# Six plain product steps at the start of a fused Fourier-mixing and SiLU kernel

## The chip, the cores and the metric

The kernel runs on one core of a Trainium2 chip. Its time is the device time of one execution in microseconds (us); the medians below are over several executions.

## The reference

The input x has 8 batches of 3008 rows and 256 channels. Each batch is mixed along its rows in the frequency domain, and every row of the result then goes through a two-layer network with SiLU. x, the filters and the result are float32; the two weight matrices come as 64-bit floats.

```python
X = np.fft.rfft(x, axis=1)                       # x: (8, 3008, 256)
Y = X * (filt_r + 1j * filt_i)[None, :, :]       # filters: (1505, 256)
y = np.fft.irfft(Y, n=3008, axis=1)
h = y.reshape(24064, 256) @ w_in                 # w_in: (256, 2048)
g = h * (1.0 / (1.0 + np.exp(-h)))
out = g @ w_out                                  # w_out: (2048, 256)
```

## The kernel before

**The mixing.** The transform of 3008 = 94 x 32 rows is done as products with small tables of cosines and sines, batch by batch. The stages have names that the profile shows as tiles: pa (along the 94), pb (along the 32), the multiplication with the filter, pc (back along the 32), pd (back along the 94), which gives y. Between stages the data is turned by writing it to DRAM and loading it in another order: t (the result of pa) goes out to d1 and comes back as t2, q (the result of pc) goes out to d2 and comes back as t4. Batch 0 is done ahead of everything else, as fast as it goes. The later batches are done in pieces between the products of the network, long before they are needed.

The x of batch 1 is laid out twice: `load_pair` and `stage1_pair` (pa for eight of the 32 columns at a time, four row groups of the array side by side; lines L422 and L432) do parts 0 to 2 ahead of the network, `load_x` and `stage1` (L379, L452) do the last two pieces, u = 6 and 7, in steps 7 and 8. `out_pair` (L445) copies pa out of PSUM, `store_rows` (L465) writes t to d1 with four DMAs of the POOL queue. `store_half` (L720) writes q to d2, `fetch_rows` (L747) loads it for pd, `stage3` (L762, copies L776) is pd of batch 0.

**The network.** The rows are handled in 48 pairs of token blocks; a pair has 8 steps (jp 0 to 7), each for 256 of the 2048 hidden units, so there are 384 steps. A step has the 2 x 2 block form of a matrix product in Winograd's variant of Strassen's scheme: seven products in place of eight at each of the two levels, and sums around them. `hidden(step)` does the first level (products at L1025 into px and pyz): it needs four differences of y, made once for each pair by `tokens` in the tile ty (on VectorE), copies of the running sum px (ScalarE, abc), sums of pyz and abc in g, and Silu (L1029). The last hidden product of a step is followed by a difference of two rows of g, and `finish` adds two more in the next step; all these sums are on VectorE through the helper `combine` (L996). `project(step)` does the second level one step later (L1093, into the accumulators acc 0 to 3, seven products from the rows of g). `drain` adds the accumulators of a pair up in the tile s (copies L1118, then seven sums on POOL), `output` stores them.

A step runs in eight rounds. In a round the generator of `hidden` and the one of `project` each issue up to their next `yield`, then come the pieces that a list has put at this step and round:

```python
for rnd in range(ROUNDS):
    held = work[1:] if rnd in ((3, 6, 7) if keeps else (0, 2) if step in opened else ()) else []
    work = [w for w in work if w in held or next(w, work) is not work]
    until(step + rnd / ROUNDS)
```

The order on each engine is therefore written out by hand. The first 16 steps take two pairs in turn, by `PARTS`: pair 0 with jp 0 and 1 (steps 0 and 1), pair 1 with jp 0 to 3 (steps 2 to 5), pair 0 with jp 2 to 7 (steps 6 to 11), pair 1 with jp 4 to 7 (steps 12 to 15).

**The weights.** They arrive as 16 blocks of 64-bit floats, two blocks for each jp, and are turned into 32-bit floats on the chip while the first steps run: `bits` (two operations of VectorE, L1222 and L1224), `converted` (two of ScalarE, L1231 and L1232), `added`, `signed` and `placed` (one of VectorE each, L1238, L1243, L1250). `combine_weights(jp)` then makes the sums of weight blocks (S1, S2, S3, S4) that the seven products need, in four operations, on VectorE for jp 0 and mostly on POOL for the others. The slot of S3 in `w_t` holds the plain block A21 until then. `weights(j)` issues the load of a block on the SP queue (L1204), into rooms that other tiles leave.

The waits between engines follow from the tiles: whoever takes a buffer over waits for its last reader, and an engine and a DMA queue do their instructions in order.

Of the kernel before, what the change touches and what calls it, by code (L numbers as in the profile page):

```python
# [46 lines left out]
FP32 = mybir.dt.float32  # L47
# [18 lines left out]
LAG = 1  # L66
PARTS = (0, 0, 2), (1, 0, 4), (0, 2, 8), (1, 4, 8)
# [55 lines left out]
def second_pairs(x):  # L123

    rows = np.zeros((96, 32, C), x.dtype)
    rows[0:NR] = x.reshape(NR, 32, C)
    return rows.reshape(3, 32, 4, 4, 2 * C).transpose(2, 3, 1, 0, 4)[0:3].reshape(3, 128, 6 * C)
# [145 lines left out]
def kernel(  # L273
# [96 lines left out]
    def spectral(b):  # L370
# [44 lines left out]
        def load_pair(p):  # L415
# [3 lines left out]
            else:  # L419
                pool, tag = (spool, "s") if p == 1 else (gpool, "g")  # L420
# [4 lines left out]
        def stage1_pair(p):  # L425
# [8 lines left out]
            if p == 2:  # L434
                t = s1pool.tile([128, 2, 2, 2, C], FP32, name=f"t1_{b}_{p}", tag="s1")
                t = [t[:, i] for i in range(2)]
            else:
                pool, tag = (tpool, "t") if p else (typool, "ty")
# [23 lines left out]
        def store_rows(u):  # L462
            t1 = us.pop(("t1", u))
            for k in range(4):
                nc.gpsimd.dma_start(out=d1[k // 2, :, k % 2, 4 * u:4 * u + 4],  # L465
                                    in_=t1[32 * k:32 * k + NS].rearrange("p h n c -> p (h n) c"))

# [364 lines left out]
        return dict(us=us, store_half=store_half, load_pair=load_pair, stage1_pair=stage1_pair, out_pair=out_pair, store_rows=store_rows, evict_y=evict_y, halves=halves, load_first=load_first, stage1_first=stage1_first, load_x=load_x, stage1=stage1, reverse_x=reverse_x,  # L832
# [15 lines left out]
    def plan(b, part):  # L848
# [3 lines left out]
        if b == 1:  # L852
            for u in range(6, 8):
                put(at + u - 47, 3, part["stage1"], u)
        else:
# [203 lines left out]

    def finish():  # L1060
# [9 lines left out]

    def project(step):
# [4 lines left out]
        if new:  # L1076
            acc[pair] = {}
        last = step == n_steps - 1 or steps[step + 1][0] != pair

        order = PROJECT  # L1080
# [4 lines left out]
        elif new:  # L1085
# [3 lines left out]
        for c, k, i, h in order:  # L1089
            if i not in acc[pair]:  # L1090
# [3 lines left out]
                             start=(new and h == 0), stop=last, skip_group_check=True)  # L1094
            if last and pair == len(pairs) - 1:
                drain_last(pair, i, h, n, acc[pair])
            elif last and (h == 1 or i == 3):
                drain(pair, i)
            yield
# [3 lines left out]
    def drain(pair, i):  # L1103
        n = pairs[pair][3]
        more = (pair, i) in parts
        if i == 0 and not more:
# [4 lines left out]
        if i < 3:  # L1111
            dst, src = s[:, 2 * i:2 * i + 2, 0:n], acc[pair][i][:, :, 0:n]
        else:
            dst, src = s[:, 6, 0:n], acc.pop(pair)[3][:, 0, 0:n]
        if more:
# [6 lines left out]
        if i < 3:  # L1122
            return
# [431 lines left out]
```

## Time and profile before

| | |
|---|---|
| median of 3 runs | 2499.14 us (2498.75 to 2501.53) |
| the profiled execution | 2500.93 us |
| its span in the profile | 2499.1 us |
| mean granted clock of TensorE | 0.998 |
| PE products of L1093 and L1025 | 5376 records each |
| HBM read and written | 96.06 MB and 81.26 MB, 71 GB/s over the span |

PE is TensorE, PEld its weight loads, DVE is VectorE, ACT is ScalarE, POOL is GpSimd; SPq, ACTq and POOLq are the queues on which these engines issue DMAs. Times in the profile are counted from the start of the span. A product of two float32 matrices appears as two records of PE. Lines (L1025) are those of the kernel before; in the changed kernel they are some lines further down.

### The profile page before, as it was taken

The page shows a single profiled execution, that of the slowest core. Times are in us where ns is not written, and L with a number is a line of the kernel's source. Part 1 is how long each engine was busy: PE and PEld are TensorE (multiplying, and loading weights), DVE is VectorE, ACT ScalarE, POOL GpSimd, SP SyncE. Part 2 cuts the span into 40 slices and gives each one's busy share as a digit, 9 for nine tenths or more (in the row PEclk, how much of TensorE's full clock was granted, in tenths as well). Part 3 has the DMA queues.
Part 4 walks back from the last instruction along what each step waited for, and adds up shares of the span by engine and source line. Part 5 has one row for each costly group of instructions (what it writes and reads, how often), then busy time and mean ns, then how long its engine had stood idle before and what let it go on. Part 6 is the DMA issues. An engine that isn't in the chain of part 4 may idle for free.

```text
span 2499.1 us, 42322 instructions
## 1 busy us (share of the span) xinstructions
PE 2479.1 (99%) x16234; PEld 2125.2 (85%) x16234; DVE 1761.5 (70%) x3593; ACT 1092.3 (44%) x3001; POOL 458.4 (18%) x708
## 2 busy tenths in 40 slices
PE   9999999999999999999999999999999999999999
PEld 6778888888888888888888888889888888888988
DVE  7876677777777777777777867777677767655544
ACT  3634444444444444444444444444444444444443
POOL 4421112112121122211122112211221111101100
PEclk9999999999999999999999999999999999999999
DMA  8433233213242032420333203321142211200000
GB/s 303 147 88 103 67 72 82 72 37 81 60 96 72 23 93 53 114 63 20 82 75 100 55 26 91 79 68 43 35 107 54 56 43 35 63 21 9 17 9 17
DMA packets 139771, 170.68 MB, mean 68 GB/s; under 512 B 21053, under 2 KB 113565, under 8 KB 139037
## 3 DMA queue, kind: packets, MB, share of 16 engines
q1 hardware_dynamic: 115952, 121.15, 18.4%
q0 software_dynamic: 22656, 45.68, 7.0%
q8 instruction: 127, 2.08, 0.3%
q10 hardware_dynamic: 960, 1.16, 0.1%
q14 instruction: 76, 0.61, 0.1%
HBM read 96.06 MB, written 81.26 MB: 71 GB/s over the span
## 4 chain that ended last, share of the span: by engine, by line
PE 96%; DVE 2%; ACT 0%; issue 0%; POOL 0%; DMA 0%; DVEq 0%; POOLq 0%
PE acc L1093 45%; PE px L1025 25%; PE pyz L1025 19%; PE pd L800 1%; PE pf L522 1%; PE pc L618 1%; PE pb L580 1%; DVE g L996 1%; PE pc L696 0%; PE pa L402 0%; PE pb L562 0%; PE pd L762 0%; PE pa L432 0%; PE idle L1322 0%; DVE w_t L1250 0%
## 5 line engine op out<-in xcount | busy, mean ns | idle before, releaser
L1093 PE MATMUL acc<-g,w_t 128*128 128x256 f32 (+1 forms) x5376 | 1508.6, 376 | 3.2 <-ACT o L813 2.5
L1093 PEld LDWEIGHTS acc<-g,w_t 128*128 128x128 f32 x5376 | 1017.1, 190 | 153.5 <-ACT o L813 15.3
L996 DVE TENSOR_TENSOR g<-pyz,abc 128x256 f32<-128x256 f32 (+1 forms) x1152 | 479.6, 416 | 471.3 <-ACT abc L1046 231.4
L996 DVE TENSOR_TENSOR g<-g 128x256 f32<-128x256 f32 (+3 forms) x1152 | 591.2, 513 | 197.1 <-ACT g L1029 184.0
L1025 PE MATMUL px<-ty,w_t 128*128 128x256 f32 (+1 forms) x2304 | 677.5, 376 | 1.0 <-DVE ty L996 0.5
L1029 ACT ACTIVATE g<-g 128x256 f32<-128x256 f32 (+1 forms) x1152 | 472.8, 411 | 242.5 <-DVE g L996 242.5
L996 POOL TENSOR_TENSOR s<-s 128x256 f32<-128x256 f32 (+1 forms) x329 | 252.3, 784 | 1403.6 <-DVE s L1118 1044.8
L1025 PEld LDWEIGHTS px<-ty,w_t 128*128 128x128 f32 x2304 | 435.5, 190 | 55.9 <-issue 1.8
L1025 PE MATMUL pyz<-y,w_t 128*128 128x256 f32 (+1 forms) x1536 | 453.0, 377 | 6.6 <-DVE g L996 6.4
L1025 PEld LDWEIGHTS pyz<-y,w_t 128*128 128x128 f32 x1536 | 283.0, 190 | 52.9 <-DVE g L996 12.1
L1040 ACT COPY abc<-px 128x256 f32<-128x256 f32 (+1 forms) x384 | 141.3, 368 | 371.2 <-PE px L1025 371.2
L1046 ACT COPY abc<-px 128x256 f32<-128x256 f32 (+1 forms) x384 | 141.4, 368 | 311.6 <-PE px L1025 311.5
L1029 ACT ACTIVATE g<-px 128x256 f32<-128x256 f32 (+1 forms) x384 | 145.7, 380 | 299.3 <-PE px L1025 299.3
L1025 PE MATMUL px<-y,w_t 128*128 128x256 f32 (+1 forms) x768 | 227.8, 378 | 1.2 <-ACT g L1029 1.1
L1025 PE MATMUL pyz<-ty,w_t 128*128 128x256 f32 (+1 forms) x768 | 226.0, 376 | 0.0
L1025 PEld LDWEIGHTS px<-y,w_t 128*128 128x128 f32 x768 | 143.4, 189 | 24.9 <-ACT g L1029 3.9
L1025 PEld LDWEIGHTS pyz<-ty,w_t 128*128 128x128 f32 x768 | 142.5, 190 | 20.8 <-DVE g L996 0.6
L1033 ACT COPY abc<-px 128x256 f32<-128x256 f32 (+1 forms) x384 | 135.1, 352 | 35.2 <-PE px L1025 35.0
L542 POOL DMA_DIRECT2D d<-tf x96 | 48.7, 507 | 212.9 <-DVE tf L472 212.9
L1118 ACT COPY s<-acc 128x512 f32<-128x512 f32 (+1 forms) x94 | 54.2, 577 | 47.3 <-issue 28.5
L639 POOL DMA_DIRECT2D d<-low x36 | 22.1, 614 | 285.8 <-DVE low L635 275.1
L512 DVE TENSOR_TENSOR uf<-x_all 120x512 f32<-120x512 f32 (+1 forms) x72 | 60.2, 864 | 0.3 <-issue 0.3
(133 smaller groups left out, 1364.3 us busy)
## 6 DMA issues: line engine op xcount, KB each, us to landing
t<-d SPq DMA_DIRECT2D x84, 256.0 KB
t<-d SPq DMA_DIRECT2D x224, 96.0 KB
out_dram<-s SPq DMA_DIRECT2D x64, 256.0 KB
d<-q POOLq DMA_DIRECT2D x48, 256.0 KB, 5.2
x_all<-in_x_dram SPq DMA_DIRECT2D x96, 96.0 KB
x_all<-xr SPq DMA_DIRECT2D x96, 96.0 KB
d<-tf POOLq DMA_DIRECT2D x96, 96.0 KB, 2.7
d<-tq POOLq DMA_DIRECT2D x96, 96.0 KB, 2.8
```

The costliest lines, as they stand in the source:

```text
L512: nc.vector.tensor_tensor(out=out, in0=in0, in1=in1, op=op)
L522: nc.tensor.matmul(out=ps[q][32 * k:32 * k + 32], lhsT=wq_t[rows, k], rhs=rhs[k][rows], start=True, stop=True)
L542: nc.gpsimd.dma_start(out=d1[par, :, grp, at:at + 4], in_=part[rows].rearrange("p q n c -> p (q n) c"))
L580: nc.tensor.matmul(out=ps[k, ri][32 * j:32 * j + 32, a, :], lhsT=dn_t[rows, 4 * (g + a) + at, :], rhs=t2s[g + a][rows, at, :], start=True, ...
L996: eng.tensor_tensor(out=out, in0=in0, in1=in1, op=op)
L1025: nc.tensor.matmul(out=out, lhsT=w_t[:, jp, c, 0], rhs=rhs, start=start, stop=True, skip_group_check=True)
L1029: nc.scalar.activation(out=g[:, k, 0:n], in_=g[:, k, 0:n] if src is None else src, func=AFT.Silu)
L1033: nc.scalar.copy(out=sums[:, 0, 0:n], in_=xo)
L1040: nc.scalar.copy(out=sums[:, 1, 0:n], in_=xo)
L1046: nc.scalar.copy(out=sums[:, 2, 0:n], in_=xo)
L1093: nc.tensor.matmul(out=acc[pair][i][:, h, 0:n], lhsT=w_t[:, jp, OUT_PLACE.get(c, c), 1], rhs=g[:, k, 0:n], start=(new and h == 0), stop=la ...
L1118: copy(out=dst, in_=src)
```

## The change

- Steps 0 to 5 use a plain form: `hidden_plain` has eight products a step, two for each of four outputs, and Silu from PSUM; it needs no ty, no abc and no sum on VectorE. Their `project` has eight products in the order of `PROJECT_PLAIN`, from four rows of g. `drain` handles the banks that only one of the two forms fills, and an eighth sum on POOL joins the two forms.
- All of pa of batch 1 is done ahead of the network: `load_pair(3)` and `stage1_pair(3)` take the place of `load_x(6)`, `load_x(7)` and the two `stage1`; the products of part 3 stand between the second and the third group of pd.
- t is stored behind pd: a copy on POOL into `gate` waits for the last eviction of pd, and all stores of t, with those of q, follow it; parts 0 and 3 are stored in four DMAs of twice the size.
- Loads and tiles change place for that: x of part 2 is loaded later, into the room of part 1 before, weight block 3 later, blocks 4 and 5 before pd, block 6 behind it; t of part 3 uses a buffer of g, x of part 3 the other.
- The conversion of weights is spread anew over steps 0 to 8; `combine_weights` is done by VectorE throughout, its order changed so that A21 stays until the plain steps have used it. `tokens(0)` moves from ahead of step 0 to step 4, `tokens(1)` from step 1 to step 11.

```diff
+PLAIN = 6
...
-                pool, tag = (spool, "s") if p == 1 else (gpool, "g")
+                pool, tag = (spool, "s") if p == 2 else (gpool, "g")
...
+        def store_pair(p):
+            t1 = us.pop(("t1", "pair", p))
+            for k in range(4):
+                nc.gpsimd.dma_start(out=d1[k // 2, :, k % 2, 8 * p:8 * p + 8],
+                                    in_=t1[32 * k:32 * k + NS].rearrange("p a h n c -> p (a h n) c"))
...
-        if b == 1:
-            for u in range(6, 8):
-                put(at + u - 47, 3, part["stage1"], u)
-        else:
+        if b > 1:
...
+    def hidden_plain(step):
+        pair, jp = steps[step]
+        n, yt = pairs[pair][3], channels(pair)
+        px = xps.tile([128, 2, 256], FP32, name=f"px_{step}", tag="x")
+        pyz = xps.tile([128, 2, 256], FP32, name=f"pyz_{step}", tag="yz")
+        g = gpool.tile([128, 8, 256], FP32, name=f"g_{step}", tag="g")
+        g_t[step] = g
+        for k, ps, h, left, right, cols in ((0, px, 0, A11, A12, 0), (1, pyz, 0, A11, A12, n),
+                                            (3, px, 1, S3, A22, 0), (2, pyz, 1, S3, A22, n)):
+            for a, c in enumerate((left, right)):
+                nc.tensor.matmul(out=ps[:, h, 0:n], lhsT=w_t[:, jp, c, 0], rhs=yt[:, a, cols:cols + n],
+                                 start=a == 0, stop=a == 1, skip_group_check=True)
+                if a:
+                    nc.scalar.activation(out=g[:, k, 0:n], in_=ps[:, h, 0:n], func=AFT.Silu)
+                if (k, a) != (2, 1):
+                    yield
...
+    PROJECT_PLAIN = [(S3, 0, 3, 0), (S3, 1, 3, 1), (A22, 3, 3, 0), (A22, 2, 3, 1),
+                     (A11, 0, 1, 0), (A12, 3, 1, 0), (A11, 1, 2, 0), (A12, 2, 2, 0)]
...
-        order = PROJECT
+        order = PROJECT_PLAIN if step < PLAIN else PROJECT
...
-        for o, a, b in ((2, 0, 2), (5, 0, 5), (3, 5, 3), (6, 3, 6), (0, 5, 1), (4, 0, 4), (1, 3, 1)):
-            combine(gp, s[:, o, 0:n], s[:, a, 0:n], s[:, b, 0:n], ALU.add)
+        for o, a, b in ((2, 0, 2), (5, 0, 5), (3, 5, 3), (6, 3, 6), (0, 5, 1), (4, 0, 4), (1, 3, 1), (1, 1, 7)):
+            if b < 7 or (pair, 3, 1) in parts:
+                combine(gp, s[:, o, 0:n], s[:, a, 0:n], s[:, b, 0:n], ALU.add)
...
-    second["load_pair"](2)
     tables()
     products(2)
     part["forward"](4)
     inverse(1)
-    weights(3)
+    second["load_pair"](2)
...
     inverse(2)
+    weights(3)
...
-    for u in range(2):
-        second["store_rows"](u)
     second["stage1_pair"](2)
+    second["load_pair"](3)
     added(2)
     signed(0, 1)
     placed(0, 1)
-    combine_weights(0)
...
     added(3)
+    weights(4, 5)
+    idle(4)
+    early[0] += 7
+    part["stage3"](0)
     signed(2, 3)
-    idle(4)
-    part["stage3"](0)
     part["stage3"](1)
-    placed(2)
+    placed(2, 3)
+    second["stage1_pair"](3)
+    out_of(3, 0, 1, copy=act)
+    out_of(3, 2, copy=dve)
     part["stage3"](2)
     part["stage3"](3)
-    placed(3)
-    combine_weights(1, eng=gp)
-    for u in range(4, 6):
+    out_of(3, 3, copy=act)
+    weights(6)
+    gp.tensor_copy(out=gate, in_=y[0, 0][:, 0, 28:29])
+    second["store_pair"](3)
+    for g in (2, 3):
+        for i in range(2):
+            part["store_half"](g, i, 1, gp)
+    second["store_pair"](0)
+    for u in (4, 5, 2, 3):
         second["store_rows"](u)
-    for g in (2, 3, 4, 5, 0, 1):
+    for g in (4, 5, 0, 1):
...
-    weights(4, 5)
-    second["load_x"](6)
-    weights(6)
-    second["load_x"](7)
...
+            (0, 0, (weights, 7, 8)), (0, 1, (bits, 4)), (0, 2, (bits, 5)), (0, 3, (converted, 4), (added, 4)),
+            (0, 4, (added, 5)), (0, 5, (converted, 5)), (0, 6, (signed, 4), (placed, 4)),
+            (1, 0, (signed, 5), (placed, 5), (weights, 9, 10)), (1, 1, (combine_weights, 2, 0)),
+            (1, 2, (bits, 6), (added, 6)), (1, 3, (converted, 6)), (1, 4, (bits, 7), (added, 7)),
+            (1, 6, (signed, 6), (placed, 6), (converted, 7)), (2, 0, (signed, 7), (placed, 7), (weights, 11)),
...
-        step, rnd = combines[pair % per] if pair not in (1, 2) else ((1, 5), (12, 1))[pair - 1]
+        step, rnd = combines[pair % per] if pair > 2 else ((4, 3), (11, 1), (12, 1))[pair]
...
-            work.append(hidden(step))
+            work.append(hidden_plain(step) if step < PLAIN else hidden(step))
```

## The prediction

> **What bounds the kernel now.** I read the busy totals first, then the waits of TensorE, then its instructions in order of time from 40 to 160 us, then the same stretch for the other engines and the queues. Totals (engine, busy us, share, instructions):
>
> ```profile
> span 2499.1 us, 42322 instructions
> PE 2479.1 (99%) x16234; PEld 2125.2 (85%) x16234; DVE 1761.5 (70%) x3593; ACT 1092.3 (44%) x3001; POOL 458.4 (18%) x708
> ```
>
> TensorE (PE) is the bound, so a time comes off only where PE waits, runs slowly, or has less to do. All that the change touches runs before about 160 us. PE in order of time there (start, duration, line, operation; in brackets the idle time before it and its releaser):
>
> ```profile
> 50.31 3.92 PE L762 MATMUL pd<-wi_t,w_t 64*64 64x47 f32 x244
> 55.56 0.44 PE L762 MATMUL pd<-wi_t,w_t 64*64 64x47 f32 x12 [1.33 <-issue]
> ...
> 56.74 0.77 PE L1025 MATMUL px<-y,w_t 128*128 128x256 f32 x2
> 57.30 1.06 PE L1025 MATMUL pyz<-y,w_t 128*128 128x256 f32 x2
> 58.86 1.19 PE L1025 MATMUL px<-ty,w_t 128*128 128x256 f32 x2 [0.50 <-DVE ty L996]
> ...
> 64.20 0.70 PE L1025 MATMUL px<-y,w_t 128*128 128x256 f32 x2
> ...
> 72.44 0.70 PE L1025 MATMUL pyz<-y,w_t 128*128 128x256 f32 x2 [1.07 <-DVE g L996]
> ...
> 108.25 1.88 PE L452 MATMUL pa<-x_all,wx_t 96*128 96x512 f32 x4
> ...
> 130.47 0.70 PE L1025 MATMUL pyz<-y,w_t 128*128 128x256 f32 x2 [1.26 <-DVE g L996]
> ```
>
> One product is two records; from 64.73 us on, products start every 0.4325 us. Step 0 begins at 56.74, step 1 at 64.20: 7.46 us for seven products that need 3.03. The windows of one microsecond say why (busy us of PE, weight loads, DVE, ACT, POOL; then the granted clock, DMA share, GB/s):
>
> ```profile
> 56.00:57.00 1.00, 0.90 (x4) 0.52 (x4) 0.96 (x2) 0.45 (x1) 0.08 (x1) 1.00 0.63 180
> 58.00:59.00 1.00, 0.50 (x2) 0.17 (x2) 0.96 (x2) 0.00 (x0) 0.92 (x2) 0.50 0.97 344
> 63.00:64.00 1.00, 1.00 (x4) 0.67 (x3) 0.58 (x2) 0.24 (x1) 1.00 (x3) 0.50 1.01 303
> 64.00:65.00 1.00, 1.00 (x6) 0.73 (x5) 0.42 (x1) 0.59 (x3) 0.81 (x2) 0.99 1.11 279
> ```
>
> The clock is halved for all of step 0, and step 0 also waits for ty and for the ladder of copies of px. Later the waits are for VectorE (DVE), which does level sums and weight conversion together: it is busy 9.42 of the 10 us from 120 to 130.
>
> **A ledger to one marker.** The marker is the first hidden product of step 12, at 147.29. From 56.74 that is 90.55 us: 163 products (84 hidden, 79 of project) x 0.4325 = 70.5; two pa products of batch 1 at L452, 1.72 each = 3.4; two pd, one pb and their edges, 3.6. The other 13.0 are losses. By starts of steps (64.20, 70.34, 77.73, 84.34, 90.77, 97.36, 104.70, 112.73, 120.81, 128.09, 135.76) they are: step 0 4.4; step 1 0.1; step 2 1.3; steps 3 to 5 1.45; step 6 1.3; steps 7 and 8 0.55; steps 9 and 10 2.8; step 11 1.0.
>
> **Part 1, more products: +5.2.** Steps 0 to 5 get one hidden and one project product each: 12 x 0.4325.
>
> **Part 2, pa: -0.7.** The two pairs at L452 leave (-3.4). One more product of four row groups goes between pd 1 and pd 2. The three at L432 take 41.01 to 49.23, so 2.74 each. It needs its x, whose load (768 KB) now waits until DVE has placed weights 0 and 1, at 47.8. The nearest row is the first four loads of the kernel, of the same size: issued from 1.14, the first product that reads one starts at 6.28, about 5.0 us later. So x lands at about 52.6, pd 1 ends at 52.5, and I put the wait at 0.2 (0 to 1.5). The evictions of pa 2 that it needs end at 50.6 on ACT.
>
> **Part 3, the stall in pd: -1.3.** PE waited twice for nothing that the profile shows: 1.26 before 37.69, and the 1.33 above. Between them lie 381 matmul records and as many weight loads. If that is a block of instructions that came late, it was there at 55.56. In the changed program the same count is reached in the middle of pd 3, at about 56.8 (52.5 + 0.2 + 2.74 + 1.07 for pd 2 + 0.3), so nothing waits. If the block comes later still because the new load and weights 4 and 5 (1.8 MB) run then, up to 1.3 remains. [...]
>
> Step 0 so starts at 56.74 + 2.74 + 0.2 - 1.33 = 58.35.
>
> **Part 4, the losses of steps 0 to 11: 13.0 become 2.3.** A plain step needs nothing from DVE and no ty: each output is two products and a Silu of 0.42.
> - Clock: the fall to 0.50 at 57.4 came 3.2 us after the stall of 54.24. Without the stall PE has one gap of 0.7 ahead of step 0, so I take full clock. [...]
> - Step 0: its eight products take 3.46, but ACT converts weight 4 (two operations, 1.4) between its second and third Silu, and step 1's first product waits for that third one: 0.65.
> - Step 1 and 2: ACT's first Silu of step 1 writes a g buffer that held t of the last pa, so it waits for the store of it. POOL issues that store only after the last eviction of pd (about 58.3), four DMAs at 0.53: 58.8 to 60.9. Landing: 3.0 us is the median of such stores, 6.4 the worst row (issued 61.3, released POOL at 67.70). PE needs this Silu 7.6 us into step 0, at 66: no wait at the median. Behind these stores on POOL come those of q of groups 2 and 3, in whose room weight 7 is loaded: 62.0 + 2.5 landed, +0.5 issue, +4 load: 69. Then DVE's bits, ACT's conversion and the last Silu of step 1 follow; PE needs weight 7 by about 68.9. I put 0.4 (0 to 4).
> - Steps 2 to 5: DVE has for each weight 2 x 0.34 + 3 x 0.60 = 2.5, and 0.35 for each sum of weights, which leaves POOL (24 sums at 0.888 there go). With drains and ty that is 5.5 to 6.6 us of a step's 6.93. ACT has 4 x 0.42 + 2 x 1.4 = 4.5. It fits, with under 1.5 us of slack on the path bits, conversion, Silu: 0.5.
> - Steps 6 to 11: only weights 14 and 15 and two to three sets of sums are left, so DVE has 3.9 to 5.7 us of work in 6.06: 0.2 at the change of form, 0.5 for the rest.
> So 0.65 + 0.4 + 0.5 + 0.7 = 2.25, that is -10.7.
>
> **Part 5, what costs nothing.** The loads of x for pa 2 and of weight 3 go behind q stores on SP: each some 3 to 4 us later, but needed only at 46.5 and 43.0, and weight 3's load, issued at 36.3, should land by 41. Were it late, DVE's evictions of pa would be, 1 us at most. The stores of t leave POOL at 46 to 56 and free the queues for the rows of pd. All 36 POOL issues (19 us) should be done by 85; ty 0 is needed at 96, t2 and t4 at 130. POOL's eighth sum for pairs 0 and 1 (0.82) lies in POOL's idle time. After the marker the drains of pair 0 are shorter on DVE; the wait of 1.10 at 155.23 halves: -0.5.
>
> **Sum:** +5.2 - 0.7 + 0.2 - 1.3 - 10.7 - 0.5 = -7.8. The profiled execution took 2500.93 with a span of 2499.1; the median shown is 2499.14, so it was 1.8 above. Applied to the median: **2491.3 us**; a profile of the same kind would have a span near 2491.3.
>
> **Rivals.** (a) Start as before: the block still comes late, or the stall has another cause; 1.3 stays, the clock halves, and step 0's eight products take 6.9 in place of 3.5: 2491.3 + 1.3 + 3.4 = 2496.0. For it: those 1.8 MB on the queues from 48 to 56. Against: pa 3 gives the fetch 2.74 us. Chance 0.14. (b) The waits come back in the conversion: stores land at 6.4, weight 7 is 4 us late, or DVE and ACT do not keep step (at the 0.75 that the same weight operations took beside POOL, a step's DVE work is 7.5, 0.6 over, five times): 2494.3 to 2494.9 (+3.6, or +3.0). For it: the queues are full from 58 to 68 (shares 0.75 to 1.11). Chance 0.17. (c) Slower: the half clock stays on. It lasted 6.6 us in which PE was 0.5 to 1.0 busy with gaps of 0.5; the plain steps tie every second product to a Silu behind conversions on ACT, and if such gaps recur in steps 0 to 2, their 40 products cost 17.3 more: 2508.6. It decides once PE has a gap of about half a microsecond in each three. Against: the waits I count are 0.65 and 0.4 in 20 us. Chance 0.10. (d) The change does not do what it says, since the conversion and not the levels' sums held PE, and it only moves: DVE full, the losses of steps 1 to 11 stay (8.6, in place of the 1.6 that I leave them): 2491.3 + 7.0 = 2498.3. Against: DVE's five operations on g leave it, some 2.5 us a step. Chance 0.07. My forecast keeps 0.52.
>
> **Numbers.** The forecast's own range, with every unknown at its good or bad end, is 2488.5 to 2494. For eight in ten I add (a) and (b): 2488.5 to 2497.0. A measurement of this kernel can tell 0.2%, 5.0 us. Faster by more (below 2494.1): the forecast and half of (b), which lies on the bound, 0.60. Within: (a), the rest of (b) and (d), 0.30. Slower: (c), 0.10.
>
> **What would show it.** Right: step 0 starts near 58.4, granted clock 1.00 from 56 to 66, no "issue" wait in pd, plain steps 6.9 to 7.1 us apart, the first product of step 12 near 140, waits of PE on DVE below 1 us before it. Wrong: a clock of 0.50 near 60 (a, c), a wait of Silu on DMA d<-t or of DVE on raw (b), DVE over 9 of 10 us with PE waiting for Silu (d).

## The result: slower by 0.3%, and where the time went

The changed kernel takes 2508.79 us in the median of 11 runs (2503.17 to 2512.78), the kernel before 2500.49 beside it (2498.75 to 2502.42): a ratio of 1.0032, 95% interval 1.0023 to 1.0042. The forecast was 2491.3 and faster; its range ended at 2497.0. The profiled execution took 2512.07 us with a span of 2509.9, near the upper end of its runs, so two more were profiled (r1: 2510.03, r2: 2508.54); they show the same two waits.

The totals of the profile after (engine, busy us, share, instructions), with the queue that brings instructions:

```profile
span 2509.9 us, 42292 instructions
PE 2487.4 (99%) x16274; PEld 2129.7 (85%) x16274; DVE 1751.2 (70%) x3582; ACT 1086.4 (43%) x2984; POOL 435.7 (17%) x680
...
q8 instruction: 128, 2.10, 0.3%
```

PE in order of time in the changed kernel (start, duration, line, operation; in brackets the idle time before it and what ended it):

```profile
48.77 3.33 PE L433 MATMUL pa<-x,wx 32*128 32x512 f32 x22 [0.61 <-ACT t L447]
...
59.58 0.67 PE L770 MATMUL pd<-wi_t,w_t 64*64 64x47 f32 x12 [3.87 <-issue]
60.17 5.35 PE L433 MATMUL pa<-x,wx 32*128 32x512 f32 x24
65.45 2.14 PE L770 MATMUL pd<-wi_t,w_t 64*64 64x47 f32 x128
68.38 1.10 PE L1076 MATMUL px<-y,w_t 128*128 128x256 f32 x4 [0.16 <-DVE y L784]
...
77.47 0.70 PE L1076 MATMUL px<-y,w_t 128*128 128x256 f32 x2 [1.30 <-ACT g L1079]
87.68 1.22 PE L1076 MATMUL pyz<-y,w_t 128*128 128x256 f32 x2 [4.76 <-ACT g L1079]
...
119.17 0.70 PE L1030 MATMUL px<-ty,w_t 128*128 128x256 f32 x2 [1.12 <-ACT abc L1038]
```

Two places carry most of the loss. Inside pd, after 116 records, PE stands still for 3.87 us with nothing to wait for that the profile knows ("issue"); before, it was 1.33 us, after 244 records. In step 2, PE waits 4.76 us for a Silu. Behind each wait the granted clock is 0.50: pa 3 takes 5.35 us (the others take 2.86 at full clock, with their overlap), and from 87.68 to 92.76 six rows take 5.08 us that need 2.6. The windows of one microsecond (busy us of PE, weight loads, DVE, ACT, POOL; then the granted clock, the share of the DMA engines' time in use, GB/s) show the first:

```profile
56.00:57.00 1.00, 0.00 (x0) 0.00 (x0) 0.00 (x0) 0.00 (x0) 0.00 (x0) 1.00 0.92 369
58.00:59.00 1.00, 0.00 (x0) 0.00 (x0) 0.00 (x0) 0.00 (x0) 0.00 (x0) 0.71 0.02 8
60.00:61.00 1.00, 1.00 (x12) 0.60 (x10) 0.68 (x2) 0.47 (x1) 0.00 (x0) 0.50 0.07 16
```

From 56 to 59 no engine of the core works: first the DMA engines are full, then they too are idle, and PE still does not go on.

The second place, on the other engines:

```profile
71.19 2.17 POOL L728 DMA_DIRECT2D d<-q  x4
77.62 26.15 SPq L1235 DMA_DIRECT2D raw<-in_moe_w_dram  x9
85.36 0.49 DVE L1253 TENSOR_SCALAR e<-raw 128x512 uint32<-128x512 uint32 x1 [7.37 <-DMA raw<-in_moe_w_dram]
85.88 0.72 ACT L1262 ACTIVATE e<-e,bias_t 128x512 f32<-128x512 uint32 x1 [6.43 <-DVE e L1253]
```

POOL stores q at 71.2, SP may load weight 7 into its room at 77.6, DVE gets it at 85.4, ACT converts it, and behind that conversion on ACT stands the Silu for which PE waits.

**The ledger.** The first hidden product of step 12 comes at 158.64, where the forecast had 139.9. 10.0 of these 18.7 us are there when step 0 begins (68.38, forecast 58.35): the stall 3.9, the half clock in pa 3 2.5, 1.9 more than before between the start of pa and the end of pa 2, 0.9 by which pa of batch 1 began later than before, and 0.4 ahead of pd make 9.6. The other 8.7 lie in steps 0 to 11: 90.26 us where the forecast had 81.55. There the waits 0.38, 1.30, 4.76 and 1.12 and the half clock of 2.5 make 10.1, against 2.25 of losses in the forecast; the last 0.9 is spread over small gaps. Behind the marker 2351.3 us remain (2351.8 before): the half microsecond that was forecast.

### The profile page after: what moved, and what is told of

Same layout as the page of the kernel before. It is cut to its first block, busy times and chain, and to the rows that moved or that the text cites. A ratio compares the mean times of both kernels' runs of the same rounds, so it can differ in the third digit from the quotient of the medians.

```text
span 2509.9 us, 42292 instructions
## 1 busy us (share of the span) xinstructions
PE 2487.4 (99%) x16274; PEld 2129.7 (85%) x16274; DVE 1751.2 (70%) x3582; ACT 1086.4 (43%) x2984; POOL 435.7 (17%) x680
## 4 chain that ended last, share of the span: by engine, by line
PE 96%; DVE 1%; DMA 1%; ACT 1%; issue 0%; POOL 0%; SPq 0%; DVEq 0%
PE acc L1122 45%; PE px L1030 25%; PE pyz L1030 19%; PE pd L808 1%; PE pf L530 1%; PE pc L626 1%; PE pb L588 1%; PE pa L403 1%; DMA d<-q 0%; PE pc L704 0%; PE pb L570 0%; PE pd L770 0%; DMA raw<-in_moe_w_dram 0%; DVE g L1001 0%; PE pc L684 0%
## 5 line engine op out<-in xcount | busy, mean ns | idle before, releaser
L1001 DVE TENSOR_TENSOR g<-pyz,abc 128x256 f32<-128x256 f32 (+1 forms) x1134 | 471.8, 416 | 473.5 <-ACT abc L1051 230.7
L1001 DVE TENSOR_TENSOR g<-g 128x512 f32<-128x512 f32 (+1 forms) x1134 | 581.8, 513 | 193.7 <-ACT g L1034 180.8
L1030 PE MATMUL px<-ty,w_t 128*128 128x256 f32 (+1 forms) x2268 | 664.8, 375 | 1.1 <-ACT abc L1038 1.1
L1034 ACT ACTIVATE g<-g 128x256 f32<-128x256 f32 (+1 forms) x1134 | 465.4, 410 | 232.7 <-DVE g L1001 232.7
L1030 PEld LDWEIGHTS px<-ty,w_t 128*128 128x128 f32 x2268 | 427.5, 190 | 53.8 <-ACT abc L1038 1.5
L1030 PE MATMUL pyz<-y,w_t 128*128 128x256 f32 (+1 forms) x1512 | 443.9, 375 | 1.3 <-DVE g L1001 1.1
L1045 ACT COPY abc<-px 128x256 f32<-128x256 f32 (+1 forms) x378 | 139.2, 368 | 368.0 <-PE px L1030 368.0
L1051 ACT COPY abc<-px 128x256 f32<-128x256 f32 (+1 forms) x378 | 139.2, 368 | 309.3 <-PE px L1030 309.1
L1038 ACT COPY abc<-px 128x256 f32<-128x256 f32 (+1 forms) x378 | 132.9, 352 | 33.7 <-PE px L1030 33.7
L1150 ACT COPY s<-acc 128x512 f32<-128x512 f32 (+2 forms) x96 | 54.5, 568 | 49.3 <-issue 27.8
```

The costliest lines, as they stand in the source:

```text
L1001: eng.tensor_tensor(out=out, in0=in0, in1=in1, op=op)
L1030: nc.tensor.matmul(out=out, lhsT=w_t[:, jp, c, 0], rhs=rhs, start=start, stop=True, skip_group_check=True)
L1034: nc.scalar.activation(out=g[:, k, 0:n], in_=g[:, k, 0:n] if src is None else src, func=AFT.Silu)
L1038: nc.scalar.copy(out=sums[:, 0, 0:n], in_=xo)
L1045: nc.scalar.copy(out=sums[:, 1, 0:n], in_=xo)
L1051: nc.scalar.copy(out=sums[:, 2, 0:n], in_=xo)
```

## The experiments

Three theories and their rivals were tried. A: the stall in pd is a block of PE's instructions that comes late because loads fill the DMA engines; the half clock follows. B, its rival: the stall belongs to the count of instructions, whatever is loaded. C: step 2 waits because weight 7 must wait for the stores of q, which POOL issues too late. E: the moved loads of x of pa 2 and of weight 3 are not free. All edits are against the changed kernel, unless said otherwise; times are medians and ratios are against the kernel before, which had 2500.8 to 2501.3 beside them.

**e1, weights 4 and 5 behind pd.**

```diff
-    weights(4, 5)
     idle(4)
...
     out_of(3, 3, copy=act)
+    weights(4, 5)
     weights(6)
```

> The changed kernel with the loads of weights 4 and 5 (1.0 MB) issued behind pd, where weight 6 is issued, and not ahead of it. Theory A (the stall of 3.87 us inside pd is the block of instructions coming late because the loads ahead of pd fill the DMA engines; the half clock behind it follows from the stall): the stall falls to 1.3 us or less, the products of pa 3 take about 2.8 us and not 5.35, and step 0 starts at 62.5 to 64.5, not 68.4; the whole some 4 to 6 us shorter than the changed kernel's 2508.8, about 2503.5. Rival B (the stall belongs to the count of instructions and not to the loads): a wait of 3 to 4 us stays at the 117th product of pd, half clock behind it, step 0 at about 68.4, time within 1.5 us of 2508.8. Either way the wait of 4.76 us in step 2 should stay.

2511.68 us, ratio 1.0041 (1.0029 to 1.0054); the stall is 3.61 us. That looks like B, but the edit had no effect: SP issued these loads at 55.04, right behind the end of pa 2 (54.98), as in the changed kernel (52.17 behind 52.10), since nothing that SP waits for stands between the two places (weight 4 waits for the room of x of pa 2, in either order). Here the place in the program delayed the loads only by what their queue waits for. e1 says nothing on A.

**e2, stores of q of groups 2 and 3 ahead of the gate.**

```diff
+    for g in (2, 3):
+        for i in range(2):
+            part["store_half"](g, i, 1, gp)
     gp.tensor_copy(out=gate, in_=y[0, 0][:, 0, 28:29])
     second["store_pair"](3)
-    for g in (2, 3):
-        for i in range(2):
-            part["store_half"](g, i, 1, gp)
```

> The changed kernel with the four stores of q of groups 2 and 3 issued on POOL ahead of the gate on y and of the store of the last pair, not behind them. Theory C (the load of weight 7 waits in SP's queue for these stores, its conversion stands ahead of a Silu on ACT, and so step 2 waits 4.76 us and the clock halves again): the load of weight 7 is issued some 7 us earlier, the wait in step 2 falls below 1 us, no half clock from 87 to 92, and the time is about 6 us shorter than 2508.8: 2502 to 2504. Rival D (what makes weight 7 late is the queue of transfers itself, or the store of t that step 1's g waits for): the load moves, but the wait in step 2 stays above 3 us, and the time within 2 us of 2508.8. The stall in pd stays at 3.9 us with its half clock either way.

2505.82 us, 1.0023 (1.0014 to 1.0032). Weight 7 is issued at 65.8 and the wait in step 2 is gone, as C has it. Part of it is back in step 1 (3.12 us, where the changed kernel has 1.30): g has the buffer of the last t there and waits for its store. That weight 7, now loaded beside this store, makes it slow was not shown:

```profile
76.96 1.22 PE L1076 MATMUL px<-y,w_t 128*128 128x256 f32 x2 [3.12 <-ACT g L1079]
```

And against the expectation, this profile has no stall in pd at all, though it has the same instructions on PE and the same loads. Its pa 2 waits 2.42 us instead, and the clock is halved from 49.1 to 59.3; weights 4 and 5, which wait for the end of pa 2, go out only at 55.4.

**e3, both edits.**

> Both edits together: the loads of weights 4 and 5 behind pd, the stores of q of groups 2 and 3 ahead of the gate. By theories A and C the gains add up: 10 to 12 us under the changed kernel, 2497 to 2499, at or a little under the kernel before (2500.5). By B and D nothing changes, about 2508. If the two are one chain (a step 0 that starts earlier finds weight 7 later still), the sum is 3 us or more below the two gains.

2506.95 us, 1.0023 (1.0014 to 1.0032); the profiled run took 2501.97. Again no stall in pd, and 2.85 us of wait in step 1. The gains of 10 to 12 us did not come: e1's half of the edit does nothing, and e2's gives part of its gain back. That two variants had no stall opened a new question: is it there in every execution? The list of the DMA queues by quarters of a microsecond answers what the waits can't: queue 8 brings PE's instructions in packets of 16 KB (2.10 MB in 128 packets for 32548 records of PE and weight loads, so 254 for each), and one sees when each packet ran (times of packets are the starts of these quarters). In the changed kernel the packet in question ran at 57.00, in the kernel before (its 1.33 us) at 53.00, in e2 at 53.75, in e3 at 53.50. The queues of the changed kernel from 51 to 57, then from 57.00 to 57.25 (packets, MB, share; q1 has the loads that SP issues):

```profile
q1 hardware_dynamic: 648, 2.00, 99.6%
q10 hardware_dynamic: 41, 0.03, 2.5%
```

```profile
q1 hardware_dynamic: 16, 0.03, 30.1%
q8 instruction: 1, 0.02, 27.4%
```

For six microseconds the loads have the engines almost to themselves; the packet comes as they end. In e2 it ran ahead of the issue of weights 4 and 5, in e3 0.6 us behind it (52.9).

**e4, the kernel before with weights 4 and 5 ahead of pd.**

```diff
     signed(2, 3)
+    weights(4, 5)
     idle(4)
...
-    weights(4, 5)
     second["load_x"](6)
```

> The kernel before with one edit: the loads of weights 4 and 5 issued ahead of pd. Theory A: its stall in pd (1.33 us, at the 245th product) grows to 2.5 us or more, or another comes at the 117th product, half clock in or behind it for 5 us or more; time 1 to 5 us above 2500.5. Rival B: the stall stays at 1.3 us and at its place; time within 1.5 us of 2500.5.

2504.08 us, 1.0016 (1.0007 to 1.0025). The stall grew from 1.33 to 3.17 us at its old place, with half clock behind it, as before; the packet ran at 57.00 and not at 53.00. Of these 4 us, 2.0 are a later start of this execution (pa of batch 1 begins at 43.03, before at 41.01). So the stall changes with the loads, with the count of instructions as it was: A, and not B, by one profile and a median 3.3 us above the kernel before. In what way is not plain: the data of the loads had nearly ended by 55, and the packet ran beside stores of t (59% of the engines' time in its quarter).

```profile
59.42 0.66 PE L762 MATMUL pd<-wi_t,w_t 64*64 64x47 f32 x12 [3.17 <-issue]
```

**e5, the loads in the old order.**

```diff
     weights(2)
+    second["load_pair"](2)
     tables()
...
     inverse(1)
-    second["load_pair"](2)
+    weights(3)
...
     inverse(2)
-    weights(3)
```

> The changed kernel with the loads of x of pa 2 and of weight 3 back at their earlier places in SP's queue. Theory E (the prediction's 'costs nothing' was wrong: the moved loads delay the stores of q, the fetch that ACT waits for before it copies pa, and so pa 2): the fetch on ACT is issued some 3 us earlier, the wait of pa 2 for the copies of t (0.6 us in the changed kernel, 1.9 to 2.4 in e1 to e3) goes, and pa 2 starts 1 to 2 us earlier; 1 to 2 us off the 2508.8. But by theory A the block inside pd still waits for the end of the traffic, so the stall is as long or longer and step 0 starts no earlier: then the time stays within 1.5 us. Rival: pa 2 is held by something else, and nothing moves.

2507.06 us, 1.0022 (1.0013 to 1.0031). E holds: no wait in pa 2, and from the first pa to the first pd 9.7 us, where the changed kernel had 11.6 (before: 9.3). All eight profiles with the new order of loads show this wait, 0.3 to 2.4 us; none with the old order does. As A had it, the packet still comes after the loads (55.75) and the stall is longer, 4.72; against the expectation, step 0 begins 2.0 us earlier than in the changed kernel (66.40, there 68.38). The medians are 1.7 us apart, and their intervals overlap. The lines of pd:

```profile
51.42 2.07 PE L770 MATMUL pd<-wi_t,w_t 64*64 64x47 f32 x116
58.21 0.66 PE L770 MATMUL pd<-wi_t,w_t 64*64 64x47 f32 x12 [4.72 <-issue]
```

The old order has a price too: a stall of 0.7 to 1.3 us in pc at about 38 us, in all ten of its profiles (that of the kernel before is the first, 1.26), and in none of the new order. There too a packet (36.0 in e5, 35.0 in the changed kernel) ran later beside these loads.

**e8, weights 4, 5 and 6 behind the load of wi,** which truly waits for pd.

```diff
-    weights(4, 5)
     idle(4)
...
-    weights(6)
...
     nc.sync.dma_start(out=wi_t, in_=wi_dram.ap())
+    weights(4, 5)
+    weights(6)
```

> The changed kernel with the loads of weights 4, 5 and 6 issued behind the load of wi, which waits for the last product of pd; in e1 the loads were still issued at 55.0 us, so e1 took nothing away from ahead of pd. Theory A: the packet of 16 KB that brings the next instructions of PE lands by about 54 and not at 57.0; no wait inside pd of over 1.3 us in this profile, full clock in pa 3, step 0 at 61 to 64. What comes back: weight 4 is converted in step 0 and lands 3 to 4 us after step 0 begins, so a Silu of step 0 or 1 waits 2 to 4 us, and the stores of t and q collide with these loads, so the wait for g in step 1 and the one in step 2 grow by 1 to 3 us: 2503 to 2508. Rival B (count alone): the wait of 3.9 us inside pd stays, and the time is 2509 to 2514.

2507.4 us, 1.0022 (1.0013 to 1.0031). No stall, the packet at 52.50, full clock in pa 3, step 0 at 61.77, as A had it. And all of it given back: waits of 3.18 and 0.41 in step 1, since weight 4 is now late, and of 2.66 in step 2.

**e9, the old order of loads, and the stores held only until the first copy of pa 3.**

```diff
-    gp.tensor_copy(out=gate, in_=y[0, 0][:, 0, 28:29])
-    second["store_pair"](3)
+    gp.tensor_copy(out=gate, in_=second["us"]["t1", 6][:, 0, 0, 0:1])
     for g in (2, 3):
         for i in range(2):
             part["store_half"](g, i, 1, gp)
+    second["store_pair"](3)
```

with the edit of e5.

> The changed kernel with the old order of loads (as in e5) and, on POOL, the stores of q of groups 2 and 3 and then of the last pair held back only until the first copy of pa 3 (about 61 us, when the DMA engines were idle), not until pd is done. Theory C: weight 7 loads some 5 us earlier and the stores of t land some 3 us earlier, so the waits of step 1 (1.30, and 3.12 in e2) and step 2 (4.76) are both under 1 us, with no half clock from 87 to 92; step 0 to the first hidden product of step 12 takes 82 to 84 us, not 90.3. The stall inside pd stays (theory A), 2 to 4 us with half clock behind it where it falls so. Time 2500 to 2503. Rival: the waits of steps 1 and 2 belong to the plain form itself (buffers of g) and stay: 2506 to 2509.

2498.96 us, 0.9988 (0.9979 to 0.9997): under the kernel before, and 8.1 us under e5, from which only the stores part it. From step 0 to step 12 it takes 83.3 us (68.70 to 151.97), as C had it: the waits of steps 1 and 2 are 1.44 and none, and the clock is 1.00 from 86 to 94. The profiled execution was its longest (2505.32), with the longest stall of all, 5.22 us.

**e10, e9 and e8 together.**

> e9, and the loads of weights 4, 5 and 6 behind the load of wi as in e8. If A and C both hold and weight 4 is not too late: no stall inside pd, full clock, step 0 at 59 to 61, and 83 to 87 us from there to step 12 (weight 4 and weight 7 now load behind one another, so one Silu wait of 2 to 4 us is expected back): 2494 to 2499, below the kernel before (2500.8). If the weights behind wi cost more than the stall did, it is slower than e9.

2502.74 us, 1.0006 (0.9997 to 1.0015). The stall is down to 1.66, the clock full, step 0 at 61.84; but weight 4 comes late and holds a Silu as in e8, and half clock follows from 69 to 75. The last branch of the expectation: the weights behind wi cost more than the stall.

```profile
55.76 0.44 PE L770 MATMUL pd<-wi_t,w_t 64*64 64x47 f32 x12 [1.66 <-issue]
...
69.15 1.22 PE L1076 MATMUL px<-y,w_t 128*128 128x256 f32 x2 [3.62 <-ACT g L1079]
```

**e12, e9 with weights 4 and 5 issued from ACT in the middle of pd.**

```diff
-    weights(4, 5)
     idle(4)
...
     part["stage3"](1)
+    weights(4, 5, queue=nc.scalar)
```

> e9, with the loads of weights 4 and 5 issued from ACT behind the copies of y of the second quarter of pd (about 56.5 us): behind the packet of instructions that e8 and e10 had at 52.5 and 53.3, and still some 5 us ahead of their conversion in step 0. Theories A and C: the wait inside pd is at most 1.7 us, as in e10, with full clock in pa 3; step 0 at 59 to 62; no wait over 1.5 us in steps 0 to 2; 82 to 84 us from step 0 to the first hidden product of step 12, which then comes at 142 to 145 (147.3 in the kernel before). Time 2494 to 2497, below e9 (2499.0) and the kernel before (2501.3). Rival: the next block of instructions, asked for at about 56, now waits for these loads, and a wait of 2 us or more comes in the second half of pd: 2498 to 2501.

2499.3 us, 0.9986 (0.9978 to 0.9995). No stall at the old place (packet at 51.00). But the rival came too, at half its size: the next packet ran at 58.25, and 1.02 us of stall, where the rival had 2 or more, comes in the second half of pd. The 2494 to 2497 that were expected were missed. In step 1 g waits again for the store of t, which was issued from 62.9 on and released ACT at 72.9:

```profile
60.80 0.80 PE L770 MATMUL pd<-wi_t,w_t 64*64 64x47 f32 x36 [1.02 <-issue]
...
73.38 0.70 PE L1076 MATMUL px<-y,w_t 128*128 128x256 f32 x2 [3.07 <-ACT g L1079]
```

**e14, the stores of e9 alone.**

> The changed kernel with the order of stores of e9 alone: q of groups 2 and 3 and then the last pair, held until the first copy of pa 3; the loads as in the changed kernel. Theory C by itself: the wait of 4.76 us in step 2 and the half clock behind it go, 6 to 8 us off the 2508.8: 2501 to 2503. Rival: the 8 us between e5 and e9 came only together with the order of loads; then 2505 or more.

2503.15 us, 1.0002 (0.9994 to 1.0011), 5.6 under the changed kernel: C by itself, a little less than expected. The wait of 4.76 in step 2 and its half clock are gone; the stall (2.99) and the half clock in pa 3 (5.50) stay.

**e7, the plain form alone:** e12, with pa 6 and 7 of the second batch in the steps again.

```diff
-    second["load_pair"](3)
...
-    early[0] += 7
...
-    second["stage1_pair"](3)
-    out_of(3, 0, 1, copy=act)
-    out_of(3, 2, copy=dve)
...
-    out_of(3, 3, copy=act)
-    weights(6)
-    gp.tensor_copy(out=gate, in_=second["us"]["t1", 6][:, 0, 0, 0:1])
+    gp.tensor_copy(out=gate, in_=y[0, 0][:, 0, 4:5])
...
-    second["store_pair"](3)
...
     nc.sync.dma_start(out=wi_t, in_=wi_dram.ap())
+    second["load_x"](6)
+    weights(6)
+    second["load_x"](7)
...
-        if b > 1:
+        if b == 1:
+            for u in range(6, 8):
+                put(at + u - 47, 3, part["stage1"], u)
+        else:
```

> e12 without the second part of the change: pa 6 and 7 of the second batch are made in the steps, as in the kernel before, and there is no last pair to store. What is left of the change is the plain form of steps 0 to 5. The prediction priced pa in pd at 0.7 us less than in the steps, and charged it a wait of 0.2: then e7 is 0 to 2 us above e12, 2495 to 2499, and the wait for g in step 1 (for the store of t) is gone. Rival: pa 3 inside pd costs more than it brings, since its x is 0.8 MB of the traffic that holds the block of instructions up; then e7 is 1 to 3 us below e12.

2501.36 us, 1.0000 (0.9991 to 1.0008). That is 2.1 above e12, a little over the 0 to 2 expected, so pa 3 in pd seems worth its place. But e7 also loads weight 6 behind wi, and what it shows of the plain form alone is no more than that nothing is left of its gain in this arrangement: its steps wait 0.39, 1.69 and 1.97 us for Silus that stand behind conversions (DVE waits 2.37 and 2.44 for weights that landed late), and pd has two short stalls (0.66 and 1.59). The wait for the store of t is gone, as expected.

**e13, e12 with weights 7 and 8 issued late in step 0.**

```diff
-            (0, 0, (weights, 7, 8)), (0, 1, (bits, 4)), ...
+            (0, 1, (bits, 4)), ...
-            (0, 6, (signed, 4), (placed, 4)),
+            (0, 6, (signed, 4), (placed, 4), (lambda: weights(7, 8, queue=nc.scalar),)),
```

> e12, with the loads of weights 7 and 8 issued from ACT late in step 0 (about 68 us) and not at its start from SP (62.8 in e12). In e12 step 1 waited 3.07 us, since its g has the buffer of the last pair of t, whose store was issued at 62.9 and landed at 72.9 beside these loads. If the store is slow because of them, it lands by 69, the wait in step 1 falls below 1.5 us and the time by 1.5 to 3 us: 2496 to 2498. If the store is slow for another reason (weight 6, its own form), the wait stays near 3 us and the time within 1 us of e12. Should weight 7 land after 81, step 2 gets a wait of its own.

2500.87 us, 0.9998 (0.9989 to 1.0007). The wait in step 1 is cut up (1.50 and 0.71), but the store of t still releases ACT only at 72.27, and the two issues take time on ACT (an issue there took 0.46 and 0.61 us in the changed kernel, at 42.60 and 47.48). This does not clear the loads: with 7 and 8 out of its queue, SP issued weights 9 and 10, which are of the same size, at 62.0 and 62.5 in their place (in e12 at 63.9 and 64.9). What makes this store slow stays open.

**r1 and r2, the changed kernel again; r3 and r4, e9 again.**

> The changed kernel unchanged, a second profiled execution. Its runs lie between 2503.2 and 2512.8 us. If the late block of instructions is what parts them, an execution near 2504 shows no wait inside pd or one under 1.5 us, with full clock in pa 3, and one near 2510 the wait of 3 to 5 us; the wait of 4.8 us in step 2 is in both.

> The changed kernel unchanged, a third profiled execution: as for the second.

> e9 unchanged, a second profiled execution; the first, at 2505.3, was its slowest run, with 5.2 us of wait inside pd. One near 2497 should show that wait 3 us or more shorter, or the half clock behind it gone; the waits of steps 1 and 2 under 1.5 us as before.

> e9 unchanged, a third profiled execution: as for the second.

r1 (2510.03) and r2 (2508.54) have the stall, 3.85 and 3.25 us, with packets at 54.25 and 57.00, and step 2's wait, 5.17 and 4.51. r2 has no half clock in pa 3. No execution near 2504 was among them, so whether the stall parts the runs of the changed kernel was not seen. r3 and r4 (2495.80, 2495.68) have no stall in pd: their packets ran at 48.25 and 48.00, some 0.8 us after x of pa 3 was issued and ahead of weights 4 and 5 (49.1 and 48.9). The longest and the shortest execution of e9, the same program, first the one of 2505.32, then r4:

```profile
60.29 0.67 PE L770 MATMUL pd<-wi_t,w_t 64*64 64x47 f32 x12 [5.22 <-issue]
...
68.70 1.10 PE L1076 MATMUL px<-y,w_t 128*128 128x256 f32 x4 [0.16 <-DVE y L784]
```

```profile
49.95 2.23 PE L770 MATMUL pd<-wi_t,w_t 64*64 64x47 f32 x128
52.98 2.86 PE L433 MATMUL pa<-x,wx 32*128 32x512 f32 x24 [0.80 <-DMA x<-in_x_second_dram]
...
58.70 1.10 PE L1076 MATMUL px<-y,w_t 128*128 128x256 f32 x4 [0.16 <-DVE y L784]
```

Their 9.6 us are all there when step 0 begins, at 68.70 and at 58.70: among them 5.2 of stall, 2.1 of half clock in pa 3, and 2.7 by which pa of batch 1 began later (43.23 and 40.53). The packet of r4, from 48.00 to 48.25, did not need empty queues:

```profile
q10 hardware_dynamic: 39, 0.03, 56.9%
q1 hardware_dynamic: 15, 0.03, 48.7%
q8 instruction: 1, 0.02, 29.0%
```

The packets side by side (us; "end of pa 2" is the end of its last product; the block before begins some 0.6 to 1.0 us ahead of that):

| run | packet | end of pa 2 | PE goes on | stall | step 0 |
|---|---|---|---|---|---|
| changed | 57.00 | 52.10 | 59.58 | 3.87 | 68.38 |
| r1 | 54.25 | 49.62 | 56.90 | 3.85 | 65.97 |
| e5 | 55.75 | 50.28 | 58.21 | 4.72 | 66.40 |
| e9, longest | 57.75 | 51.62 | 60.29 | 5.22 | 68.70 |
| e10 (weights behind wi) | 53.25 | 50.88 | 55.76 | 1.66 | 61.84 |
| e12 (weights held) | 51.00 | 51.15 | | none | 62.37 |
| r4 (e9, shortest) | 48.00 | 48.81 | | none | 58.70 |

From the quarter of the packet to the next product it is 2.5 to 2.7 us in each row with a stall (2.56 for the 1.33 us of the kernel before). Where the packet runs near the end of pa 2, the block is there in time; where it runs 4.5 to 6.1 us later (all profiles), PE stands for about 3 us or more. With weights 4 and 5 loaded ahead in the changed kernel, seven of eleven profiles have the late packet, which ran as the data of these loads ended; in the other four it ran ahead of their issue (e2, r3, r4) or 0.6 us behind it (e3). With these loads held back (e7, e8, e10, e12, e13) no stall is over 1.7 us.

## Why the prediction failed, step by step

**Part 1 (more products)** stands: the plain steps that nothing disturbs are 6.9 us apart, as sixteen products of 0.4325 need.

**Part 2 (pa)** was probably right in its sign: e7 against e12 gives 2.1 us in the medians, where 0.5 was counted, but the two intervals just overlap and e7 differs in more than pa. The wait for x is 0.80 where it can be seen (r4), inside its 0 to 1.5; from issue to product it is 5.7 us there (47.26 to 52.98), where the forecast took 5.0.

**Part 3 (the stall) is the step that failed first.** Its reading of the stall, a block of instructions that came late, fits every run, and so does the count: the stalls of pc and pd lie at only three places in the order of PE's products, 253 and 128 apart, which with as many weight loads is two blocks and one of the 254 records that a packet brings here (some records are missing). The inference was wrong: "in the changed program the same count is reached at about 56.8, so nothing waits" took the time 55.56 of the one block that was late before as if blocks came by the clock. Each block is brought by a packet of its own (127 of them in the profile before, 128 after). In the kernel before, the block ahead of it had come at 49.25, while stores of t and the rows for pd were moving (DMA share 0.92); in the changed one that block, 128 products and their weight loads earlier, had to come while 1.8 MB of x and weights were moving, and it came at 57.0. The sentence after it ("if the block comes later still because the new load and weights 4 and 5 run then, up to 1.3 remains") named the cause and then bounded it by the old stall: the bound should have been the end of that traffic, about 57, plus the 2.5 us that the old stall could have shown (53.00 to 55.56). The term was -1.3; it measured +2.5, and +2.5 of half clock with it. That these loads bring the packet late is shown by e4 (57.00, before 53.00) and by the runs with the loads held back (no stall over 1.7 us); in what way they do is open. Where the block is in time, the step is right: r4 starts step 0 at 58.70, forecast 58.35.

**Part 4 (losses 13.0 to 2.3).** *Clock:* full clock was taken, since without the stall there is no gap. With two waits of 3.87 and 4.76 us there were two stretches of half clock, which cost some 5 us together. (The fall of the kernel before came at 57.18, with a granted clock of 0.59 from 57 to 58: 2.9 us after the wait began at 54.24, where the forecast has 57.4 and 3.2.) *Weight 7: 0.4 (0 to 4).* The chain was right, link by link: stores of t on POOL, stores of q behind them, weight 7 in their room, DVE, ACT, Silu. Measured from step 0 the stores of q went out as forecast (2.8 to 5.0 us in, forecast 3.7). Two sizes were wrong: from the end of their issues to the issue of the load it was 4.3 us (73.36 to 77.62) and not 3.0, and from there to DVE 7.7 and not 4, with full queues (DMA share 0.75 to 0.98 in windows of four microseconds from 70 to 86). The upper end had been worked out with one delay at a time; together they made 4.76, and the half clock behind it was in no price. *Step 1:* the wait for the store of t, "none at the median", is 1.30. *Steps 2 to 5* came out at no loss that can be seen after 92.8; 0.5 was too dear. *Step 6* waits 1.12 at the change of form, 0.2 was forecast. Without stall and late weight 7 (r4), steps 0 to 11 take 83.55 us: 2.0 above the forecast of 81.55, so that -10.7 measures -8.7 there.

**Part 5 ("costs nothing")** was wrong on the loads that were moved: 1.9 us up to the end of pa 2, because ACT has to wait for stores of q before it issues its own load (47.48, before 44.69) and copies pa behind that. "Needed only at 46.5 and 43.0" looked at who reads the data, and not at what else passes through the same queues. The half microsecond behind the marker is right.

**The rivals and the range.** (a), the late block with half clock, and (b), weight 7 late, both happened, (a) at 6.4 us (stall and half clock in pa 3) for a price of 4.7, (b) at 7.3 (wait and half clock) for 3.6, while the range took each alone. They need not be independent: both are transfers that the change has put beside others. The number came out near rival (c), 2508.6, but by luck and not by (c): after 92.6 us the granted clock is 1.00 up to 160, through waits of up to 1.12 us.

**The whole.** Against the forecast, 17.5 us are missing in the median. By the ledger of the profile (18.7), stall and late weight 7, each with its half clock, are 6.4 and some 6.9 of them (7.3 less the 0.4 that was forecast), the moved loads 1.9. Of the 8.3 us by which the changed kernel lies above the one before, the order of stores alone takes back 5.6 (e14: ratio 1.0002, the changed kernel 1.0032). With that and the old order of loads (e9) the change is what it was meant to be in the executions where the block is in time, 2495.7 (r3, r4), and 0.12% (0.03 to 0.21) under the kernel before in all. e9 and e12 are the best versions found; the 0.3% that was forecast was not reached in the median of either.

## What to carry to other kernels

A stall with no releaser that keeps its place in the count of instructions, or moves in it by whole blocks (here some 254 records, weight loads included), can be a block of instructions that came late: look in the list of DMA queues for the packet that brought it, and allow for its coming only when the loads issued around it end, as in seven of the eleven profiles with weights 4 and 5 ahead. When a change moves DMAs, draw for each queue what now runs at the same time, instructions among it, and ask of each transfer who stands behind it, not only who reads it. And an edit in program order need not move a transfer: where its queue waited for nothing in between, in e1, the loads still went out right behind the end of pa 2 (55.04 behind 54.98); check the issue time in the trace before reading the result.

## What the hardware showed that was not expected

- Instructions came late beside loads of data. The packet of 16 KB ran up to 6.1 us after the end of pa 2, as the data of weights 4 and 5 ended, and PE went on 2.5 to 2.7 us after it. When a packet is asked for is not in the trace, so that it was held up is inferred from the runs in which it came early. Full engines alone do not hold it: in e12 it ran at 51.00, in r3 at 48.25, with DMA shares of 1.01 and 1.15 in these microseconds. Nor did it run at every opening: in e1 the engines were at 0.01 from 55.5 to 56.0, and it ran at 59.50. Whether the late packets waited or were asked for late was not shown.
- A block came late though the queues ahead of its packet were nearly empty. In the kernel before, the block ahead of the 1.33 us began at 52.08, the packet ran at 53.00 (DMA share 0.07 from 52 to 53, 0.68 in the microsecond after), and PE went on at 55.56: 3.5 us for one block, while 128 products of pd take 2.1 to 2.2.
- Half clock does not go by the length of the gap alone: it came behind waits of 1.33 (before), 1.89 (e1), 2.4 (e2, e3, e8), 3.17 (e4) and 3.87 us, and did not behind 1.66 (e10), 3.07 (e12) and 3.25 us (r2). In the clock records of the profiles before and after, the changes of the clock from its first rise to its last lie whole multiples of 3.413 us apart: 51.20 and 6.83 us before, 47.79, 6.83, 20.48 and 6.83 after. The three stretches of half clock there, behind the waits of 1.33, 3.87 and 4.76, last 6.83 us each. Whether the place of a gap between such points decides was not tested.
- The same program starts differently. pb begins its second part at 19.4 to 22.2 us in these profiles, since the clock first becomes full at 4.9 to 10.7 us and the first products of pa run at half speed till then (in the changed kernel, full from 10.6, they take 1.0 to 1.1 us each up to 10.5 and 0.59 from 11 on). In r3 and r4 (full from 5.4 and 4.9) the packet came ahead of the loads, in the longest execution of e9 (10.6) behind them; but r1, full from 5.2, has the late packet too, so that this shift decides it was not shown.
